# Hash attention and a gated feed-forward on one core: one token order for all batches, a longer hold on loads, and another end of the first and last block

## The chip, the cores and the metric

The kernel runs on one core of a Trainium2 chip. The metric is the device time of one execution in microseconds; before the change the median of five runs is 347.8 us (346.58 to 350.35). TensorE is called PE here, VectorE DVE, ScalarE ACT, GpSimd POOL and SyncE SP, as in the profile.

## The reference

```
B, H, S, D = 4, 8, 768, 64                       # q, k, v; proj is 64 x 6
q_bits = (einsum('bhsd,dk->bhsk', q, proj) > 0)  # the same for k
q_bucket = sum(q_bits * 2 ** arange(6), -1)
mask = q_bucket[:, :, :, None] == k_bucket[:, :, None, :]
scores = where(mask, matmul(q, k^T) / sqrt(D), -1e9)
attn = exp(scores - max); attn /= sum(attn) + 1e-9
x = (attn @ v).transpose(0, 2, 1, 3).reshape(3072, 512)
g = x @ w_gate                                   # 512 x 1536
ffn = (gelu(g) * (x @ w_val)) @ w_out
out = x + sigmoid(x @ w_res) * ffn
```

## The kernel before

**Tiles.** A batch has 768 tokens, six tiles of 128. Work goes by head pairs: 16 of them, n = 0 to 15, n = 4 b + j. For each pair, "aug" holds q and k transposed (64 rows) and under them seven rows made of the hash bits, so that one matmul over 71 rows gives score and mask together, and exp on ACT, with no maximum taken off, gives the weights. The matmul "attend" (L627) multiplies the weights with v, to which a column of ones is appended, so that the row sums come along; they collect in one PSUM tile "av" (a ring of one buffer) that has both heads of the pair side by side. DVE then takes the reciprocal of the sums (L640) and multiplies (L641) into "xtok", tokens by features.

**Blocks.** The queries are split in two halves, c = 0 and 1, of 384 tokens. A batch and a half make a block u = 2 b + c, eight in all. A block has 24 steps (`LB`): four head pairs, two heads, three pairs of key tiles (`steps`). Attention of block u runs woven with the feed-forward (`feed_forward`) of block u - 1: the value half (L697) with DVE's multiply (L700), then for each of three token tiles the residual gate (L709, tanh at L712) and the output (L721, then L730 and L733 on DVE and a store, L740). At the end of a block (`end_block`) the rest of that feed-forward is flushed, and then come twelve `gate` calls: four matmuls each (L681) and a gelu on ACT (L685), for which ACT loads another table.

**xT.** The feed-forward needs x transposed, "xT". In block 0 this is done by PE (L663, `transpose_x`) and a copy (L669), in the others by a DMA transpose of each head pair, issued on SP (L649) as soon as the pair's xtok is there. The gate takes its four contraction tiles, one for each head pair, in two parts, so that all but the last can begin before the last pair has arrived.

**Loads.** q, k, v of batch 0 come with tokens p*6+t (partition p, tile t), and its key tiles are taken in the order 0, 2, 4, 1, 3, 5 (`TS`). The pairs 4 to 15 are loaded by `load_blocks` on SP: four DMAs for q and four for k, each 32 columns of one head into 32 partitions (24 blocks of 32 tokens by 32 columns, 128 bytes a packet), and one for v. DVE turns each 32 by 32 block (L550), which makes the transpose. In these batches token t*128+p lies at partition p of tile t. POOL casts v (L403) and moves the hash bits by DMA (L568). Staging has three buffers each for q, k and v.

**Order.** Every operation is first listed by `op` with a cost, the keys that it reads and writes, and a place in the list. `arrange` then simulates the five engines and gives each the first listed operation that is ready. `urgent` moves an operation forward; `opens` and `closes` start and end a hold: while "xfer" is held, operations marked `held` on SP and POOL that are listed after the one that opened it aren't placed. It is opened by the exp of the seventh step from a block's end and closed by the block's last DMA transpose. For the loads the planner books 0.8 us of wire for a part of q or k and 1.8 for v. It also puts small matmuls into gaps of PE before 35 us (`keep_warm`, L850 and L853).

Of the kernel before, what the change touches and what calls it, by code (L numbers as in the profile page):

```python
# [11 lines left out]
FP32 = mybir.dt.float32  # L12
BF16 = mybir.dt.bfloat16
# [7 lines left out]
def kernel(  # L21
# [17 lines left out]
    P = 128  # L39
# [99 lines left out]
    def bank(dtype=FP32):  # L139
        return ring("mm", [P, 512 if dtype == FP32 else 1024], dtype, PSUM)  # L140
# [136 lines left out]
    def load(name, eng, queue, dst, cols, src, size, cost=0.5, held=False):  # L277
        queue_of = {"SP": nc.sync, "ACT": nc.scalar, "POOL": nc.gpsimd}
        op(eng, cost, lambda: queue_of[eng].dma_start(cols(dst()), src), r=[(name + "s", "gate")], w=[(dst, queue)],
           size=size, held=held)  # L280
# [18 lines left out]
    def load_blocks(n):  # L299

        b, j = pairs[n]
        for nm, src in (("q", q), ("k", k)):
            s = stage_of(nm, n, [P, S // Q, Q])
            for hh in range(2):
                for c in range(D // Q):
                    g = hh * D + c * Q
                    load(nm, "SP", g, s, lambda t, g=g: t[g:g + Q],
                         src[b, 2 * j + hh, :, c * Q:(c + 1) * Q].rearrange("(m p) d -> p m d", p=Q), 0.8, 0.85, True)
        s = stage_of("v", n, [P, 2, T, D])
        load("v", "SP", 0, s, lambda t: t, v[b, 2 * j:2 * j + 2].rearrange("h (t p) d -> p h t d", p=P), 1.8, held=True)  # L310


    for nm in "qk":
# [266 lines left out]
             for hh in range(2) for jp in range(T // 2)]  # L580
    LB = NPAIR * 2 * (T // 2)
    LEAD = 2
    URG, AVM = 200, 0.4
    PS = 2 * (T // 2)
    x_tok, xT, gh = {}, {}, {}
    e_tiles, av_tiles = {}, {}
# [2 lines left out]
    def scores(i):  # L589
        b, c, j, hh, jp = steps[i]  # L590
        n = b * NPAIR + j
        a = aug_of(n)[0:KAUG, hh, :]
        sp = ring("sc", [P, 2, 512], FP32, PSUM)
        e = e_tiles[i] = ring("e", [P, 2, CH], BF16)

        def emit():
            for x in range(2):
                jt = 2 * jp + x
                nc.tensor.matmul(sp()[:, x, 0:CH], a[:, S + jt * P:S + (jt + 1) * P],  # L599
                                 a[:, c * CH:(c + 1) * CH], start=True, stop=True)  # L600
        keys = [(0, c)] + sorted({(1, (2 * jp + x) // TC) for x in range(2)})
        op("PE", 0.325, emit, r=[("aug", n % NAUG, hh, side, p, kind) for side, p in keys for kind in "db"], w=[sp])
        op("ACT", 0.72, lambda: nc.scalar.activation(e(), sp()[:, :, 0:CH], AF.Exp, scale=EXPS),  # L603
           r=[sp], w=[e], table="exp", held=True, opens=("pair", i // PS) if i % PS == PS - 1 else None)
        if i % LB == LB - 1:
            ops[-1].opens = ("block", i // LB)
        if i % LB == LB - 7 and i // LB:
            ops[-1].opens = ("xfer", i // LB)

    def attend(i):  # L610
        b, c, j, hh, jp = steps[i]
        u = i // LB
        e = e_tiles.pop(i)
        first = hh == 0 and jp == 0
        last = hh == 1 and jp == T // 2 - 1
        if first:
            av_tiles[0] = ring("av", [P, 512], FP32, PSUM)
        av = av_tiles[0]
        va = vaugs[b % 2]

        def emit():
            live[:] = [] if last else [av]
            for x in range(2):
                jt = 2 * jp + x
                for t in range(TC):
                    o = (hh * TC + t) * DV
                    nc.tensor.matmul(av()[:, o:o + D + 1], e()[:, x, t * P:(t + 1) * P],  # L627
                                     va[:, 2 * j + hh, TS[b][jt], :],
                                     start=(first and x == 0 and t == 0), stop=(jt == T - 1),
                                     skip_group_check=True)  # L630
        op("PE", 0.18, emit, r=[e, ("vaug", b % 2, j)], w=[av], margin=AVM if first and u == 0 else 0.0)
        if last:
            if j == 0:
                x_tok[u] = ring("xtok", [P, NPAIR, TC, P], BF16)
            xt = x_tok[u]
            rec = ring("rec", [P, 2, TC, 1], FP32)

            def view():
                return av()[:, 0:2 * TC * DV].rearrange("p (h t d) -> p h t d", h=2, d=DV)
            op("DVE", 0.23, lambda: nc.vector.reciprocal(rec(), view()[:, :, :, D:D + 1]), r=[av], w=[rec], urgent=URG if u == 0 else 0)  # L640
            op("DVE", 0.56, lambda: nc.vector.tensor_mul(  # L641
                xt()[:, j].rearrange("p t (h d) -> p h t d", h=2),
                view()[:, :, :, 0:D], rec().to_broadcast([P, 2, TC, D])), r=[av, rec], w=[(xt, j)],
               closes=("pair", i // PS), urgent=URG if u == 0 else 0)
            if u:
                if j == 0:
                    xT[u] = ring("xT", [P, KM, CH], BF16)
                x = xT[u]
                op("SP", 1.25, lambda: nc.sync.dma_start_transpose(x()[:, j, :].rearrange("p (t n) -> p t n", n=P), xt()[:, j].rearrange("p t d -> p (t d)")),  # L649
                   r=[(xt, j)], w=[(x, j)], flight=2.0, closes=("xfer", u) if j == NPAIR - 1 else None)  # L650

# [21 lines left out]
    def gate(u, m):  # L673
        if m == 0:
            gh[u] = ring("gh", [P, KF, CH], BF16)
        g, x = gh[u], xT[u]
        ps = bank()
        for part in ((0, 1), (2, 3)) if u == 0 else ((0, 1, 2), (3,)):
            def emit(part=part):
                for kk in part:  # L680
                    nc.tensor.matmul(ps()[:, 0:CH], wg[:, kk, m * P:(m + 1) * P], x()[:, kk, :],  # L681
                                     start=(kk == 0), stop=(kk == KM - 1))
            op("PE", 0.163 * len(part), emit, r=[(key, kk) for kk in part for key in (x, "wg")], w=[ps],
               opens=("gelu", u) if m == 0 else None)
        op("ACT", 0.385, lambda: nc.scalar.activation(g()[:, m, :], ps()[:, 0:CH], AF.Gelu),  # L685
           r=[ps], w=[(g, m)], table="gelu", closes=("gelu", u) if m == 0 else None)

    def feed_forward(u):
# [14 lines left out]
        for t in range(TC):  # L703
# [11 lines left out]
            for h, W in enumerate(parts):  # L715
                cols = slice(sum(parts[:h]), sum(parts[:h]) + W)
                ps = bank()
                for k4 in range(KF // 4):
                    def emit(t=t, k4=k4, ps=ps, cols=cols, W=W):
                        for kk in range(4 * k4, 4 * k4 + 4):  # L720
                            nc.tensor.matmul(ps()[:, 0:W], g()[:, kk, t * P:(t + 1) * P], wo[:, kk, cols],  # L721
                                             start=(kk == 0), stop=(kk == KF - 1))
                    op("PE", 0.87 * W / DMODEL, emit, r=[(g, kk) for kk in range(4 * k4, 4 * k4 + 4)] + [("wo", gg) for gg in range(KF // 3)],
                       w=[ps], over=True)
                    if k4 < KF // 4 - 1:
                        yield 0.87
                z = "z" if len(parts) > 1 else ""
                y = ring("y" + z, [P, parts[0]], FP32)
                o = ring("o" + z, [P, parts[0]], FP32)
                op("DVE", 0.1 + 0.56 * W / DMODEL, lambda y=y, th=th, ps=ps, cols=cols, W=W: nc.vector.scalar_tensor_tensor(  # L730
                    y()[:, 0:W], th()[:, cols], 1.0, ps()[:, 0:W], op0=ALU.add, op1=ALU.mult), r=[th, ps], w=[y],
                   closes=("block", u + 1) if t == TC - 1 else None)
                op("DVE", 0.1 + 0.58 * W / DMODEL, lambda y=y, o=o, t=t, cols=cols, W=W: nc.vector.scalar_tensor_tensor(  # L733
                    o()[:, 0:W].rearrange("p (j d) -> p j d", d=P), y()[:, 0:W].rearrange("p (j d) -> p j d", d=P), 0.5,
                    xt()[:, cols.start // P:cols.stop // P, t, :], op0=ALU.mult, op1=ALU.add),
                   r=[y] + [(xt, j) for j in range(NPAIR)], w=[o])
                lay = "(p t) d -> p t d" if b == 0 else "(t p) d -> p t d"
                dst = out[b * S:(b + 1) * S, cols].rearrange(lay, t=T)[:, TS[b][c * TC + t], :]
                eng, queue = ("SP", nc.sync) if u == 2 * B - 1 else ("POOL", nc.gpsimd)
                op(eng, 0.6, lambda o=o, dst=dst, W=W, queue=queue: queue.dma_start(dst, o()[:, 0:W]), r=[o], size=0.8)  # L740
            yield 0.87
# [151 lines left out]
```

## Time and profile before

| | |
|---|---|
| five runs | 346.58, 346.87, 347.80, 349.71, 350.35 us |
| profiled execution | 346.87 us, span 345.1 us |
| PE clock | 1.00 throughout |
| PE, ACT, DVE, POOL busy | 98%, 68%, 56%, 18% of the span |
| DMA packets | 116357, of which 107802 under 512 bytes |
| DMA transposes | 28, 1.2 us each on SP when the queue is quiet |

The span runs from the first instruction to the last; the time of the execution holds 1.8 us more around it. Times in a timeline are microseconds from the start of the span. A line of a timeline has the start, the length (of all that is merged into it), engine, line, operation, tiles and count, and in brackets the idle time before it and what ended it.

### The profile page before, as it was taken

Reading aid. Unit: us, or ns where it says so; the run is one execution under the profiler, and the core shown is the slowest. Engines: PE = TensorE matmul, PEld = TensorE weight load, DVE = VectorE, ACT = ScalarE, POOL = GpSimd, SP = SyncE. Lnnn points to the kernel's source line nnn. Section 1 sums busy time; section 2 is a strip of 40 time slices with the busy share of each in tenths; the row PEclk is TensorE's granted clock in tenths of the full one; section 3 lists DMA queues with packets and bytes.
Section 4 is the critical chain, followed back from the end, with each engine's and each line's share of the span. In section 5 each row is a group of like instructions: output and inputs, shape, how many; then the busy total and the mean of one; then the engine's idle time right before and its main releaser. Section 6 shows DMA issues by size and latency. Waiting matters only on the chain.

```text
span 345.1 us, 7720 instructions
## 1 busy us (share of the span) xinstructions
PE 337.2 (98%) x3088; PEld 200.5 (58%) x3088; DVE 192.1 (56%) x344; ACT 234.2 (68%) x338; POOL 61.9 (18%) x107
## 2 busy tenths in 40 slices
PE   8999999989999999999999999999999999999996
PEld 3756666546555566555665556655666556655654
DVE  5997056977789738895453326725153314423353
ACT  4879887566766587666867758675877858775410
POOL 0444000540334310314011210203000100001000
PEclk9999999999999999999999999999999999999999
DMA  7999999999997399948200210111000120112002
GB/s 237 343 220 208 198 144 162 169 172 177 152 154 96 79 188 164 121 105 148 46 13 17 77 45 2 28 44 49 30 13 13 45 74 0 24 43 74 0 2 91
DMA packets 116357, 34.23 MB, mean 99 GB/s; under 512 B 107802, under 2 KB 113698, under 8 KB 116322
## 3 DMA queue, kind: packets, MB, share of 16 engines
q1 hardware_dynamic: 109522, 22.27, 42.3%
q0 software_dynamic: 6496, 11.27, 13.8%
q8 instruction: 24, 0.39, 0.5%
q10 hardware_dynamic: 304, 0.20, 0.2%
q14 instruction: 11, 0.09, 0.1%
HBM read 29.36 MB, written 6.29 MB: 103 GB/s over the span
## 4 chain that ended last, share of the span: by engine, by line
PE 87%; DVE 4%; DMA 4%; ACT 3%; issue 1%; DVEq 0%; ACTq 0%
PE mm L697 18%; PE mm L681 17%; PE sc L599 16%; PE mm L721 15%; PE av L627 9%; PE mm L709 5%; DMA xT<-xtok 4%; PE mm L558 3%; ACT e L603 2%; PE idle L850 1%; PE mm L481 1%; PE mm L518 1%; DVE bits L445 1%; PE mm L494 0%; DVE xtok L641 0%
## 5 line engine op out<-in xcount | busy, mean ns | idle before, releaser
L603 ACT ACTIVATE e<-sc 128x768 bf16<-128x768 f32 x192 | 149.9, 810 | 52.3 <-PE sc L599 51.9
L700 DVE TENSOR_TENSOR gh<-mm,gh 128x384 bf16<-128x384 f32 x96 | 53.4, 557 | 78.1 <-PE mm L697 62.8
L599 PE MATMUL sc<-aug 71*128 71x384 bf16 x384 | 92.3, 325 | 1.0 <-ACT e L603 0.9
L697 PE MATMUL mm<-xT,wv 128*128 128x384 bf16 x384 | 73.3, 326 | 0.0
L627 PEld LDWEIGHTS <-e 128*128 128x128 bf16 x1152 | 57.1, 97 | 24.3 <-issue 1.9
L721 PE MATMUL mm<-wo,gh 128*128 128x512 bf16 (+2 forms) x312 | 70.8, 363 | 0.0
L681 PE MATMUL mm<-xT,wg 128*128 128x384 bf16 x384 | 66.4, 326 | 1.8 <-DMA xT<-xtok 1.4
L685 ACT ACTIVATE gh<-mm 128x384 bf16<-128x384 f32 x96 | 45.5, 491 | 29.7 <-PE mm L681 29.5
L627 PE MATMUL av<-vaug,e 128*128 128x65 bf16 x1152 | 62.7, 193 | 0.6 <-DVE xtok L641 0.6
L681 PEld LDWEIGHTS <-wg 128*128 128x128 bf16 x384 | 36.9, 98 | 26.9 <-issue 2.7
L599 PEld LDWEIGHTS <-aug 71*128 71x128 bf16 x384 | 34.7, 98 | 28.7 <-issue 4.6
L697 PEld LDWEIGHTS <-wv 128*128 128x128 bf16 x384 | 34.0, 98 | 21.5 <-issue 3.1
L721 PEld LDWEIGHTS <-gh 128*128 128x128 bf16 x312 | 27.2, 98 | 24.6 <-issue 0.6
L730 DVE SCALAR_TENSOR_TENSOR y<-th,mm 128x512 f32<-128x512 bf16 x23 | 15.7, 684 | 43.6 <-PE mm L721 39.1
L568 POOL DMA_DIRECT2D aug<-bits x48 | 26.9, 564 | 67.5 <-DVE bits L565 66.8
L740 POOL DMA_DIRECT2D out_dram<-o x21 | 12.4, 592 | 133.3 <-DVE rec L640 112.6
L712 ACT ACTIVATE th<-mm 128x512 bf16<-128x512 f32 x24 | 14.3, 597 | 16.5 <-PE mm L709 16.5
L573 DVE TENSOR_SCALAR aug<-trT 64x1536 bf16<-64x1536 f32 x24 | 24.4, 1017 | 1.1 <-PE sc L599 0.4
L709 PE MATMUL mm<-wr,xT 128*128 128x512 bf16 x96 | 24.7, 379 | 0.0
L403 POOL CAST vaug<-vs 128x768 bf16<-128x768 f32 x16 | 13.3, 833 | 46.2 <-DMA vs<-in_v_dram 32.2
L565 DVE TENSOR_SCALAR bits<-mm,shift 128x384 bf16<-128x384 f32 x24 | 13.6, 609 | 9.7 <-PE mm L558 9.5
L641 DVE TENSOR_TENSOR xtok<-av,rec 128x384 bf16<-128x384 f32 x32 | 17.8, 557 | 1.1
(58 smaller groups left out, 166.6 us busy)
## 6 DMA issues: line engine op xcount, KB each, us to landing
vs<-in_v_dram SPq DMA_DIRECT2D x16, 384.0 KB
out_dram<-o POOLq DMA_DIRECT2D x21, 256.0 KB, 2.4
qs<-in_q_dram SPq DMA_DIRECT2D x48, 96.0 KB
ks<-in_k_dram SPq DMA_DIRECT2D x48, 96.0 KB
wg<-in_moe_w_gate_dram POOLq DMA_DIRECT2D x4, 384.0 KB, 7.4
wv<-in_moe_w_val_dram POOLq DMA_DIRECT2D x4, 384.0 KB, 8.1
wo<-in_moe_w_out_dram POOLq DMA_DIRECT2D x4, 384.0 KB, 12.5
qs<-in_q_dram SPq DMA_DIRECT2D x3, 384.0 KB
```

What stands on the lines that cost most here:

```text
L568: op("POOL", 0.6, lambda i=i: nc.gpsimd.dma_start(a[D:KAUG, :, i * CH:(i + 1) * CH], bits()[32 * i:32 * i + NR]), r=[(bits, 0), (bits, 1)] ...
L573: lambda hh=hh: nc.vector.tensor_scalar_mul(a[0:D, hh, :], trT()[hh * D:(hh + 1) * D].rearrange("d s n -> d (s n)"), QKS),
L599: nc.tensor.matmul(sp()[:, x, 0:CH], a[:, S + jt * P:S + (jt + 1) * P], a[:, c * CH:(c + 1) * CH], start=True, stop=True)
L603: op("ACT", 0.72, lambda: nc.scalar.activation(e(), sp()[:, :, 0:CH], AF.Exp, scale=EXPS), r=[sp], w=[e], table="exp", held=True, opens=(" ...
L627: nc.tensor.matmul(av()[:, o:o + D + 1], e()[:, x, t * P:(t + 1) * P], va[:, 2 * j + hh, TS[b][jt], :], start=(first and x == 0 and t == 0 ...
L641: op("DVE", 0.56, lambda: nc.vector.tensor_mul(xt()[:, j].rearrange("p t (h d) -> p h t d", h=2), view()[:, :, :, 0:D], rec().to_broadcast ...
L681: nc.tensor.matmul(ps()[:, 0:CH], wg[:, kk, m * P:(m + 1) * P], x()[:, kk, :], start=(kk == 0), stop=(kk == KM - 1))
L685: op("ACT", 0.385, lambda: nc.scalar.activation(g()[:, m, :], ps()[:, 0:CH], AF.Gelu), r=[ps], w=[(g, m)], table="gelu", closes=("gelu", u ...
L697: nc.tensor.matmul(ps()[:, 0:CH], wv[:, kk, m * P:(m + 1) * P], x()[:, kk, :], start=(kk == 0), stop=(kk == KM - 1))
L700: op("DVE", 0.46, lambda m=m, ps=ps: nc.vector.tensor_mul(g()[:, m, :], ps()[:, 0:CH], g()[:, m, :]), r=[ps], w=[(g, m)])
L709: nc.tensor.matmul(rps(), x()[:, kk, t * P:(t + 1) * P], wr[:, kk, :], start=(kk == 0), stop=(kk == KM - 1))
L721: nc.tensor.matmul(ps()[:, 0:W], g()[:, kk, t * P:(t + 1) * P], wo[:, kk, cols], start=(kk == 0), stop=(kk == KF - 1))
```

## The change

Loads of pairs 4 to 15 take tokens p*6+t, as batch 0 does; a part of q or k becomes a pattern of four indices, v one of longer rows, and the stores of all batches use the one pattern. The planner books 1.15 us of wire for v. In block 1 the hold "xfer" opens nine steps from the end in place of seven. In block 0, the last pair's reciprocal and multiply are done for each head as soon as it is there, and the planner tracks "av" by head. In the last block, the last pair is transposed on PE and copied by ACT or DVE, and the first two gates of that block take their PSUM from the ring of the scores. `SURG` is 0 and changes nothing.

```diff
-   load(nm, "SP", g, s, lambda t, g=g: t[g:g + Q],
-        src[b, 2 * j + hh, :, c * Q:(c + 1) * Q].rearrange("(m p) d -> p m d", p=Q), 0.8, 0.85, True)
+   load(nm, "SP", g, s, lambda t, g=g: t[g:g + Q].rearrange("p (t r) d -> p t r d", t=T),
+        src[b, 2 * j + hh, :, c * Q:(c + 1) * Q].rearrange("(r p t) d -> p t r d", p=Q, t=T), 0.8, 0.85, True)
-   load("v", "SP", 0, s, lambda t: t, v[b, 2 * j:2 * j + 2].rearrange("h (t p) d -> p h t d", p=P), 1.8, held=True)
+   load("v", "SP", 0, s, lambda t: t, v[b, 2 * j:2 * j + 2].rearrange("h (p t) d -> p h t d", t=T), 1.15, held=True)
...
+   XF = {1: 9}
-   if i % LB == LB - 7 and i // LB:
+   if i % LB == LB - XF.get(i // LB, 7) and i // LB:
        ops[-1].opens = ("xfer", i // LB)
...
-   op("PE", 0.18, emit, r=[e, ("vaug", b % 2, j)], w=[av], margin=AVM if first and u == 0 else 0.0)
-   if last:
+   op("PE", 0.18, emit, r=[e, ("vaug", b % 2, j)], w=[(av, hh)], margin=AVM if first and u == 0 else 0.0)
+   single = u == 0 and j == NPAIR - 1
+   if last or single and jp == T // 2 - 1:
...
+       heads = slice(hh, hh + 1) if single else slice(0, 2)
+       nh = heads.stop - heads.start
...
+       op("DVE", 0.18 + 0.025 * nh, lambda: nc.vector.reciprocal(rec()[:, 0:nh], view()[:, :, :, D:D + 1]),
+          r=[(av, h) for h in range(heads.start, heads.stop)], w=[rec], urgent=URG if u == 0 else 0)
+       op("DVE", 0.12 + 0.22 * nh, lambda: nc.vector.tensor_mul(
...
+   if u == 2 * B - 1 and j == NPAIR - 1:
+       ps = bank(BF16)
+       def emit():
+           for t in range(TC):
+               nc.tensor.transpose(ps()[:, t * P:(t + 1) * P], xt()[:, j, t, :], ident_bf)
+       op("PE", 0.2, emit, r=[(xt, j)], w=[ps])
...
+       op(None, {"DVE": 0.35, "ACT": 0.45}, evac, r=[ps], w=[(x, j)])
+       return
...
+   spare = u == 2 * B - 1 and m < 2
+   ps = ring("sc", [P, 2, 512], FP32, PSUM) if spare else bank()
...
-   lay = "(p t) d -> p t d" if b == 0 else "(t p) d -> p t d"
-   dst = out[b * S:(b + 1) * S, cols].rearrange(lay, t=T)[:, TS[b][c * TC + t], :]
+   dst = out[b * S:(b + 1) * S, cols].rearrange("(p t) d -> p t d", t=T)[:, TS[b][c * TC + t], :]
```

More of the change, by code (lines that the diff above doesn't have):

```diff
@@ L582 @@
     LEAD = 2
-    URG, AVM = 200, 0.4
+    XF = {1: 9}
+    URG, AVM, SURG = 200, 0.4, 0
     PS = 2 * (T // 2)
@@ L601, in scores @@
         keys = [(0, c)] + sorted({(1, (2 * jp + x) // TC) for x in range(2)})
-        op("PE", 0.325, emit, r=[("aug", n % NAUG, hh, side, p, kind) for side, p in keys for kind in "db"], w=[sp])
+        op("PE", 0.325, emit, r=[("aug", n % NAUG, hh, side, p, kind) for side, p in keys for kind in "db"], w=[sp],
+           urgent=SURG if i < LB else 0)
         op("ACT", 0.72, lambda: nc.scalar.activation(e(), sp()[:, :, 0:CH], AF.Exp, scale=EXPS),
@@ L635, in attend @@
             xt = x_tok[u]
+            heads = slice(hh, hh + 1) if single else slice(0, 2)
+            nh = heads.stop - heads.start
             rec = ring("rec", [P, 2, TC, 1], FP32)
             def view():
[L639 to L644, printed above, removed]
+                return av()[:, 0:2 * TC * DV].rearrange("p (h t d) -> p h t d", h=2, d=DV)[:, heads]
+            op("DVE", 0.18 + 0.025 * nh, lambda: nc.vector.reciprocal(rec()[:, 0:nh], view()[:, :, :, D:D + 1]),
+               r=[(av, h) for h in range(heads.start, heads.stop)], w=[rec], urgent=URG if u == 0 else 0)
+            op("DVE", 0.12 + 0.22 * nh, lambda: nc.vector.tensor_mul(
+                xt()[:, j].rearrange("p t (h d) -> p h t d", h=2)[:, heads],
+                view()[:, :, :, 0:D], rec()[:, 0:nh].to_broadcast([P, nh, TC, D])),
+               r=[(av, h) for h in range(heads.start, heads.stop)] + [rec], w=[(xt, j)] if last else [(xt, j, "half")],
+               closes=("pair", i // PS) if last else None, urgent=URG if u == 0 else 0)
+        if last:
+            xt = x_tok[u]
             if u:
@@ L648, in attend, with evac @@
                 x = xT[u]
+                if u == 2 * B - 1 and j == NPAIR - 1:
[4 more added lines that the diff above has]
+                    op("PE", 0.2, emit, r=[(xt, j)], w=[ps])
+                    def evac(e):
+                        copy = nc.scalar.copy if e == "ACT" else nc.vector.tensor_copy
+                        copy(x()[:, j, :], ps()[:, 0:CH])
+                    op(None, {"DVE": 0.35, "ACT": 0.45}, evac, r=[ps], w=[(x, j)])
+                    return
                 op("SP", 1.25, lambda: nc.sync.dma_start_transpose(x()[:, j, :].rearrange("p (t n) -> p t n", n=P), xt()[:, j].rearrange("p t d -> p (t d)")),
@@ L676, in gate, with acc @@
         g, x = gh[u], xT[u]
-        ps = bank()
+        spare = u == 2 * B - 1 and m < 2
+        ps = ring("sc", [P, 2, 512], FP32, PSUM) if spare else bank()
+        def acc():
+            return ps()[:, 0, 0:CH] if spare else ps()[:, 0:CH]
         for part in ((0, 1), (2, 3)) if u == 0 else ((0, 1, 2), (3,)):
@@ L680, in emit @@
                 for kk in part:
-                    nc.tensor.matmul(ps()[:, 0:CH], wg[:, kk, m * P:(m + 1) * P], x()[:, kk, :],
+                    nc.tensor.matmul(acc(), wg[:, kk, m * P:(m + 1) * P], x()[:, kk, :],
                                      start=(kk == 0), stop=(kk == KM - 1))
@@ L684, in gate @@
                opens=("gelu", u) if m == 0 else None)
-        op("ACT", 0.385, lambda: nc.scalar.activation(g()[:, m, :], ps()[:, 0:CH], AF.Gelu),
+        op("ACT", 0.385, lambda: nc.scalar.activation(g()[:, m, :], acc(), AF.Gelu),
            r=[ps], w=[(g, m)], table="gelu", closes=("gelu", u) if m == 0 else None)
```

## The prediction

> **What bounds the kernel now.** I read the page first. Its rows for one engine each, in tenths of 40 slices, say which engine is full where.
>
> ```profile
> span 345.1 us, 7720 instructions
> PE 337.2 (98%) x3088; PEld 200.5 (58%) x3088; DVE 192.1 (56%) x344; ACT 234.2 (68%) x338; POOL 61.9 (18%) x107
> PE   8999999989999999999999999999999999999996
> DVE  5997056977789738895453326725153314423353
> DMA  7999999999997399948200210111000120112002
> ```
>
> TensorE (PE) is busy everywhere; the DMA engines are full from the start to about 110 us and hardly used later. A full PE means that moving work on another engine is worth only the PE time that waits for it. So the second view is the waits of PE, all of them:
>
> ```profile
> PE mm L681 <- DMA xT<-xtok: 1.4, 1, 1.4
> PE idle L850 <- DVE proj_pair L332: 1.2, 1, 1.2
> PE sc L599 <- ACT e L603: 0.9, 3, 0.4
> PE av L627 <- DVE xtok L641: 0.6, 2, 0.3
> PE mm L681 <- ACT gh L685: 0.3, 1, 0.3
> ```
>
> These are gaps between records, and a record outlasts the issue of its matmul. One 384-column matmul is issued every 0.163 us (36 of L681 take 5.85 us in the chain of waits), though its record lasts 0.326. So I count lost issue time: start of the next matmul less start of the last, less 0.163. The timeline at the end of block 1 (the second boundary), PE and then the SP queue:
>
> ```profile
> 75.82 0.49 PE L681 MATMUL mm<-xT,wg 128*128 128x384 bf16 x2
> 77.73 1.79 PE L681 MATMUL mm<-xT,wg 128*128 128x384 bf16 x10 [1.42 <-DMA xT<-xtok]
> ...
> 64.42 2.32 SPq L279 DMA_DIRECT2D qs<-in_q_dram  x4
> 66.84 3.41 SPq L279 DMA_DIRECT2D ks<-in_k_dram  x4
> 70.37 0.46 SPq L279 DMA_DIRECT2D vs<-in_v_dram  x1
> 70.93 4.46 SPq L649 DMA_TRANSPOSE xT<-xtok  x2
> ```
>
> The second L681 starts at 75.99, the third was due at 76.15 and starts at 77.73: 1.58 us lost, to the DMA transpose of the last head pair. The same count at the other boundaries gives 0.23 at 160.2, 0.25 at 240.6, nothing at 118, 200 and 278, and 0.42 at the last one:
>
> ```profile
> 311.69 1.03 PE L709 MATMUL mm<-wr,xT 128*128 128x512 bf16 x4
> 312.55 2.75 PE L721 MATMUL mm<-wo,gh 128*128 128x512 bf16 x12
> 315.14 2.15 PE L681 MATMUL mm<-xT,wg 128*128 128x384 bf16 x12
> 317.54 0.65 PE L681 MATMUL mm<-xT,wg 128*128 128x384 bf16 x3 [0.25 <-ACT gh L685]
> ```
>
> There the last of twelve starts at 316.96, the next was due at 317.12 and starts at 317.54. From 36 us to the end this is all that PE loses to others, 2.5 us; whatever the change does there, it can't win more than 2.0 (both places it touches), 0.6%.
>
> **The load part.** A load of v goes from 1536 packets of 256 bytes to 256 of 1536. The trace has both: 256-byte packets on that queue took 23.9 ns in the mean, 1536-byte ones 71. On 16 engines that is 2.29 us against 1.14, 1.15 less for each of 12 loads. The loads of q and k keep their 6144 packets of 128 bytes a pair (18.2 ns, 7.0 us) in another order; their price in that order isn't in the trace. I take 18.2; the nearest rows bound it from 13.2 to 24.7, the lowest and highest means in 6-us stretches between 48 and 108 us, or 5.1 to 9.5 us a pair. A four-index source is what v has already, and its issue took 0.46 to 0.66 us, so issuing costs the same. None of this is on PE's path: the DMA engines run ahead, and the cover is the ring of three staging tiles. So 0, with v at 1.15 less a pair only thinning the traffic.
>
> By the Trainium skill ("DMA: Bandwidth & Descriptors", Why small descriptors are slow) a 256-byte descriptor costs 11 cycles, 3 of them overhead, so joining six would save under a quarter of v's wire time by an estimate from it, not half; the row decides, and the sum is 0 by either.
>
> The stores of batches 1 to 3 change from adjoining rows to every sixth, 2048 bytes each as before: 0.
>
> **The longer hold.** The exp that opens "xfer" in block 1 is now step 39, not 41, some 2.3 us earlier. Loads later in program order stay off SP until the block's last transpose is placed. The loads of pair 7 (listed at step 39, after its scores) are those at 64.42 to 70.83: nine DMAs, moved past the transposes of head pairs 2 and 3. Staging slots bound how many slip through: pair 7's q needs the slot of pair 4, transposed at 57.40 on DVE, and the hold opens near 60, so at most some three of nine go ahead.
>
> What that gives: pair 2's rows of xtok are done at 65.3 and needn't wait till 70.93; pair 3's are done at 72.97 and found SP in pair 2's transpose till 74.09, which took 3.15 us behind the loads instead of the 1.2 of a quiet queue. In the quiet boundary at 156 the chain shows 4.04 us from the end of DVE L641 to the landing. 72.97 + 4.05 = 77.02 instead of 77.69, so the third L681 starts 0.67 earlier: **-0.67**. Bounds: 0 if the landing stays where it is, -1.58 if DVE isn't held up by L733 ahead of L640 (it starts the reciprocal 0.7 late) and planned times fall well. What is late next: DVE, as 0.9 us of the wait stays.
>
> Where the moved loads go: they start at about 74.2, land by 74.2 + 8.1 + 3 = 85, then DVE 4, PE 0.8, POOL bits 2.3 and their landing 3.8 us: about 96, against the first use of pair 7 near 107 (step 66). Pairs 8 and later shift by some 8 us; pair 8 is first scored in block 4. So 0, covered by 11 us.
>
> **First block by head.** The last pair's reciprocal and multiply (0.20 + 0.56) become two of each. From L730's widths (512: 0.684, 256: 0.422, so 1.03 ns an element) a half multiply takes 0.36, so the tail is 0.20 shorter. But the tail isn't what PE waits for: the scores at 34.73 wait for ACT's exp that ends at 34.69, and the PE transposes follow them at 35.06, 0.2 after DVE ended. Gain 0 to 0.07. Against it stands a new wait. Both heads lie in one tile "av", and no row of before has DVE reading av while PE writes it; if DVE's read of head 0 orders the next av matmul behind it, PE waits. Head 0 ends at 31.70; DVE is then in a copy till 32.04, so its half ends at 32.3 or 32.65; the attend due at 32.17 comes at 32.45 or 32.8 (the hand-over of av took 0.14 at 30.52 to 30.66). Behind it stand fillers and the next scores, which then end at 33.24 to 33.57 for an exp due at 33.14: ACT, the bound there, loses 0.1 to 0.43. I take **+0.2**, bounds -0.1 and +0.45.
>
> The Trainium skill ("PSUM — Partial Sum Buffer", PSUM bank collisions) wants a bank guarded as a whole, not by address, which speaks for the wait; no overlap in this trace tests it. By it alone I would put +0.27, without it 0.
>
> **Last block on PE.** Three transposes at the 0.056 us of L663 (six in 0.34) add 0.17 on PE. They need xtok at 312.68 + 0.1; PE has L709 and four L721 till 313.41, so no wait. The copy out (0.35 to 0.55 as in L669, half as wide) hides behind the eight L721 that follow. The 0.42 goes, and m = 0, 1 take two score banks, idle by then. Removed from SP: one transpose with nothing behind it. **-0.42 + 0.17 = -0.25**; bounds +0.17 (the wait stays) and -0.25.
>
> **Sum.** -0.67 + 0.2 - 0.25 = -0.72. The profiled execution took 346.87 for its span of 345.1 (1.8 around it): 346.15. The median of the five runs lies 0.93 above it (346.58 to 350.35), and I can't see where the others lost that; if at the second boundary, it goes as well, if elsewhere, it stays (347.1). I say 346.5.
>
> **Rivals.**
> (1) The wait only changes hands: the landing is still late because DVE's L640 and L641 are, and the split costs its 0.4. Then -0.25 + 0.45 = +0.2: 347.1 to 347.5. For it: 0.9 of 1.58 is DVE's and the transpose's own time. Against: the SP rows show queueing of over 1 us.
> (2) Slower: DVE fills up in block 2. Pair 7's 3.85 us on DVE (two L550, two L573, at 80.02 to 83.83) leave the gate phase, where DVE is idle a third of the time, for the stretch 86 to 112, where it is busy 21.6 of 26: 25.4, 98%. The planner books 0.46 for L700, which takes 0.557: 12 x 0.097 = 1.2, and up to 0.7 for two L573. At full DVE this 1.9 falls on PE: 346.15 + 1.9 = 348.1; if all 3.85 do, 350.0. It decides once DVE passes about 98% in that stretch. Against it: pair 8's 3.9 us there aren't due until block 4 and can give way.
> (3) The hold does not bite, because the planner's queue runs ahead of the real one: 346.87 + 0.2 - 0.25 = 346.8. The slot of pair 4 speaks against it.
>
> **How the numbers follow.** Forecast 0.55, its own range 345.0 to 347.5; rival 1 0.17, rival 2 0.2, rival 3 0.08. The low end of the range is the floor, 346.87 - 1.58 - 0.25 - 0.1 = 344.9; the high end takes in half of rival 2, 348.9. A measurement of this kernel tells about 1% from no change; 1% faster (344.3) is under the floor and needs the spread of the runs to shrink too, 0.07; 1% slower (351.3) needs rival 2 in full and more, 0.08.
>
> **What would show it.** Right: SP has no q, k, v load between the transposes of head pairs 2 and 3 of block 1; the first of these is issued near 65 and lands before 70; PE's wait on xT falls from 1.4 to 0.3 to 0.9; the last boundary shows three transposes of L663's length and no wait on ACT. Wrong: a PE wait at L627 on DVE L641 or L640 over 0.5 near 32 us, PE waits on DVE between 86 and 112, or packets of 128 bytes well over 25 ns.

## The result and the profile after

The changed kernel takes 346.16 us (median of 43 executions, 345.44 to 347.32), the kernel before 347.17 (80 executions, 345.47 to 350.64); the ratio is 0.9962, 95% interval 0.995 to 0.9975. The ratios, here and below, are those on record over undisturbed executions, not quotients of the medians (here 0.9971), while medians and ranges are over all. The fastest executions of the two kernels are alike (345.44 and 345.47). What the change takes away most is the slow tail of before: 23 of 80 took more than 348 us, of the changed kernel none. The bulk moves less: the lower quartile is 346.63 before and 345.86 after.

The page of the changed kernel, as it was shown of before (a line of 40 digits has the tenths of 40 slices):

```profile
span 344.3 us, 7728 instructions
PE 337.6 (98%) x3091; PEld 200.8 (58%) x3091; DVE 191.1 (55%) x347; ACT 234.6 (68%) x338; POOL 62.4 (18%) x107
PE   8998999999999999999999999999999999999996
DVE  4998146864889638895464326725153414424353
DMA  7999998729995399826900210111000120111002
```

PE is as full as before, and the DMA engines show a hole in the ninth slice (69 to 77.5 us): the second boundary has lost its load traffic. All waits of PE:

```profile
PE idle L878 <- DVE proj_pair L332: 1.2, 1, 1.2
PE av L629 <- DVE xtok L648: 0.9, 3, 0.3
PE sc L600 <- ACT e L605: 0.9, 3, 0.4
PE mm L710 <- ACT gh L714: 0.2, 1, 0.2
```

The wait on xT, 1.4 us, is gone altogether; the attend (now L629) waits for DVE one time more. The second boundary, PE and then SP (L710 is the gate, L673 the DMA transpose):

```profile
75.99 1.14 PE L710 MATMUL mm<-xT,wg 128*128 128x384 bf16 x6
76.96 0.49 PE L600 MATMUL sc<-aug 71*128 71x384 bf16 x2
77.29 1.14 PE L710 MATMUL mm<-xT,wg 128*128 128x384 bf16 x6
...
66.49 1.21 SPq L673 DMA_TRANSPOSE xT<-xtok  x1
73.92 1.20 SPq L673 DMA_TRANSPOSE xT<-xtok  x1
75.17 1.31 SPq L279 DMA_DIRECT2D qs<-in_q_dram  x2
```

Head pair 2's transpose is issued at 66.49, 0.03 after its multiply ends and in 1.2 us, where it was issued at 70.93 and took 3.15; pair 3's at 73.92; pair 7's loads come after both. PE issues six gate matmuls, two scores and six gate matmuls without a gap.

The last boundary:

```profile
311.97 1.89 PE L750 MATMUL mm<-wo,gh 128*128 128x512 bf16 x8
313.70 0.33 PE L665 MATMUL mm<-ident_bf,xtok 128*128 128x128 bf16 x3
313.86 1.03 PE L750 MATMUL mm<-wo,gh 128*128 128x512 bf16 x4
314.73 1.46 PE L710 MATMUL sc<-xT,wg 128*128 128x384 bf16 x8
316.03 2.28 PE L710 MATMUL mm<-xT,wg 128*128 128x384 bf16 x13
```

The three transposes start 0.16 before the next group and the gates run through: the 0.42 before the thirteenth gate is gone.

### The profile page after: what moved, and what is told of

Its sections match the earlier page's. It is cut to its first block, busy times and chain, and to the rows that moved or that the text cites. A ratio compares the mean times of both kernels' runs of the same rounds, so it can differ in the third digit from the quotient of the medians.

```text
span 344.3 us, 7728 instructions
## 1 busy us (share of the span) xinstructions
PE 337.6 (98%) x3091; PEld 200.8 (58%) x3091; DVE 191.1 (55%) x347; ACT 234.6 (68%) x338; POOL 62.4 (18%) x107
## 4 chain that ended last, share of the span: by engine, by line
PE 93%; DVE 4%; ACT 1%; issue 0%; ACTq 0%; DVEq 0%
PE mm L726 18%; PE mm L750 18%; PE mm L710 17%; PE sc L600 17%; PE av L629 10%; PE mm L738 6%; PE mm L558 3%; PE idle L878 1%; PE mm L518 1%; PE mm L481 1%; ACT e L605 1%; DVE aug L455 1%; DVE aug L435 1%; PE mm L494 1%; DVE bits L445 1%; DVE xtok L648 1%
## 5 line engine op out<-in xcount | busy, mean ns | idle before, releaser
L629 PEld LDWEIGHTS <-e 128*128 128x128 bf16 x1152 | 57.2, 97 | 24.6 <-issue 2.2
L710 PE MATMUL mm<-xT,wg 128*128 128x384 bf16 x376 | 64.7, 326 | 0.2 <-ACT gh L714 0.2
L714 ACT ACTIVATE gh<-mm 128x384 bf16<-128x384 f32 x94 | 44.6, 491 | 27.9 <-PE mm L710 27.8
L629 PE MATMUL av<-vaug,e 128*128 128x65 bf16 x1152 | 62.7, 193 | 0.9 <-DVE xtok L648 0.9
L710 PEld LDWEIGHTS <-wg 128*128 128x128 bf16 x384 | 37.1, 98 | 25.1 <-issue 0.5
L741 ACT ACTIVATE th<-mm 128x512 bf16<-128x512 f32 x24 | 14.3, 597 | 16.6 <-PE mm L738 16.6
L403 POOL CAST vaug<-vs 128x768 bf16<-128x768 f32 x16 | 13.6, 850 | 65.1 <-DMA vs<-in_v_dram 59.6
L565 DVE TENSOR_SCALAR bits<-mm,shift 128x384 bf16<-128x384 f32 x24 | 13.6, 607 | 9.3 <-PE mm L558 9.2
L648 DVE TENSOR_TENSOR xtok<-av,rec 128x384 bf16<-128x384 f32 (+1 forms) x33 | 18.0, 545 | 1.1
```

Of the source, the lines that this page charges most:

```text
L648: op("DVE", 0.12 + 0.22 * nh, lambda: nc.vector.tensor_mul(xt()[:, j].rearrange("p t (h d) -> p h t d", h=2)[:, heads], view()[:, :, :, 0: ...
L710: nc.tensor.matmul(acc(), wg[:, kk, m * P:(m + 1) * P], x()[:, kk, :], start=(kk == 0), stop=(kk == KM - 1))
```

## The experiments

Lines in experiments made from the kernel before keep its numbers (L681 gate, L649 DMA transpose), those made from the changed kernel have the new ones. The experiments ran in three groups, in which the kernel before had a median of 346.91, 347.16 and 348.22 us; differences of some tenths of a microsecond between groups say little.

**One part at a time.** Theory A says that the hold does it all at the second boundary, theory B that the thinner traffic of the token order does.

hold_only, from the kernel before:

```diff
-        if i % LB == LB - 7 and i // LB:
+        if i % LB == LB - (9 if i // LB == 1 else 7) and i // LB:
```

> The kernel before with the hold of block 1 opened at step 39 and nothing else changed; in its program PE's order at the second boundary is the one of the changed kernel (six gate matmuls, two scores, six gate matmuls). Theory A (the hold alone takes away the wait of PE on xT at the second boundary, and that wait is also what spreads the runs of the kernel before from 345.5 to 350.6): median about 346.2 us, nothing above 348, no PE wait on xT near 76 us, 128-byte packets still near 18 ns. Theory B (the thinner load traffic of the new token order does it): 347.0 us, runs up to 350, a wait on xT of 1 us or more remains.

Measured: 346.20 us (345.30 to 346.71) beside 346.91 of the kernel before (345.94 to 350.44), ratio 0.996 (0.9933 to 0.9988). No wait near 76 us. 128-byte packets 17.0 ns.

layout_only, from the kernel before: the load, store and 1.15 lines of the diff alone.

> The kernel before with tokens p*6+t in all batches and 1.15 booked for v; hold as before, so PE's order at the second boundary is that of before (four scores, twelve attends, then twelve gate matmuls). Theory A: median about 347.0 us with runs up to 350, the wait of PE on xT near 76 us stays at 1 us or more. Theory B: 346.3 us and no runs above 348. Either way: v packets of 1536 bytes at 65 to 90 ns, 128-byte packets at 14 to 15 ns as in the changed kernel if their order makes them quicker, 18 if only the timing of the loads did.

Measured: 346.83 us (345.55 to 349.76), ratio 0.9968 (0.9934 to 1.0002). The wait stands:

```profile
76.06 0.49 PE L681 MATMUL mm<-xT,wg 128*128 128x384 bf16 x2
78.44 1.78 PE L681 MATMUL mm<-xT,wg 128*128 128x384 bf16 x10 [1.89 <-DMA xT<-xtok]
```

128-byte packets took 14.1 ns, v's 1536-byte ones 84.

no_hold, from the changed kernel:

```diff
-    XF = {1: 9}
+    XF = {}
```

> The changed kernel with the hold of block 1 back at seven steps. Theory A: the wait on xT near 76 us is back (1 to 1.6 us), median about 347.0 us and runs up to 350. Theory B: 346.2 us as the changed kernel, no spread.

Measured: 346.74 us (345.42 to 347.71), ratio to before 0.9965 (0.9938 to 0.9991). Theory A had 347.0, B 346.2; the median lies between and the spread comes back in part. Its profiled execution (345.81) shows a wait of 0.55 us at the second boundary. Together: the hold takes the wait away, as A says. It is worth 0.71 alone and 0.58 on top of the rest, between medians. The layout without the hold seems to thin the tail: 1 of 24 executions of layout_only and no_hold took over 348 us, against 23 of 80 before.

**What the wait is.** PE's order in the program of before at the second boundary, after four scores and twelve attends, is three gate matmuls for m = 0, three for m = 1, three for m = 2, and then the last ones. The wait stands before the third. That one needs head pair 2's transpose, not the last pair's. The chain of waits of the kernel before has it: its wait begins at 70.93, which is the issue of pair 2's transpose (pair 3's is issued at 74.19).

```profile
70.93 6.76 DMA xT<-xtok
77.73 1.79 PE mm L681 x10
```

But the hold also changes PE's order, because the planner sees pair 2 come sooner. Theory Q: the transpose stood in the queue; theory O: the other order is what helps.

hold_old_order, from hold_only:

```diff
             op("PE", 0.163 * len(part), emit, ...
+               margin=(0.5 if part == (3,) and m < 3 else 6.6 if m == 0 and part != (3,) else 0.0) if u == 1 else 0.0,
```

> hold_only with PE's order at the second boundary forced back to that of before (four scores, twelve attends, then gate matmuls 3, 3, 3, 1, 1): the planner is told that the first gate matmuls of block 1 become ready 6.6 us later and the last parts 0.5 us later. In the profiles so far the gate matmul that waits near 76 us is the third, which needs the transpose of head pair 2, not 3. Theory Q (pair 2's transpose stood in the queue behind pair 7's loads, and the hold takes it out from behind them): no wait at the third gate matmul; pair 3, landing near 78, may hold the tenth for up to 0.7 us; 346.2 to 346.9 us, nothing above 348. Theory O (the hold only helps because PE's order is another one): the third gate matmul waits 1.5 us or more again, 347.0 us, runs up to 350.

Measured: 346.49 us (345.52 to 346.97), ratio 0.9969 (0.9932 to 1.0005). The old order, no wait in it:

```profile
74.81 0.81 PE L599 MATMUL sc<-aug 71*128 71x384 bf16 x4
75.46 0.53 PE L627 MATMUL av<-vaug,e 128*128 128x65 bf16 x12
75.83 1.95 PE L681 MATMUL mm<-xT,wg 128*128 128x384 bf16 x11
```

early_old_queue, from the kernel before:

```diff
-                   r=[(xt, j)], w=[(x, j)], flight=2.0, ...
+                   r=[(xt, j)], w=[(x, j)], flight=-3.0 if u == 1 and j == 2 else 2.0, ...
```

> The kernel before, where the planner alone is told that pair 2's transpose of block 1 lands 5 us sooner: SP's order is as before (pair 7's loads ahead of the transpose), PE's order at the boundary is nearly that of the changed kernel (six gate matmuls right after the outputs). Theory Q: the third gate matmul is due about 1 us sooner and its data come no sooner: it waits 2.2 to 2.8 us; four scores less stand before it, so the time is as before or worse, 347.0 to 348.2 us, with runs up to 351. Theory O: no wait, 346.2 us.

Measured: median 348.83 us of ten executions, ratio 1.0012 (0.9968 to 1.0056). Nine took 345.31 to 350.60, one 1852.45, and why that one did is not known. The median is above what theory Q gave (347.0 to 348.2). PE, then SP:

```profile
75.29 0.49 PE L681 MATMUL mm<-xT,wg 128*128 128x384 bf16 x2
78.46 0.81 PE L681 MATMUL mm<-xT,wg 128*128 128x384 bf16 x4 [2.68 <-DMA xT<-xtok]
...
64.89 2.31 SPq L279 DMA_DIRECT2D qs<-in_q_dram  x4
67.31 3.49 SPq L279 DMA_DIRECT2D ks<-in_k_dram  x4
70.93 0.45 SPq L279 DMA_DIRECT2D vs<-in_v_dram  x1
71.48 4.23 SPq L649 DMA_TRANSPOSE xT<-xtok  x2
```

The new order with the old queue waits longer: the third gate is due at 75.62 and comes at 78.46, 2.84 us lost. The old order with the new queue doesn't wait, and none of its ten executions took over 347 us. Theory Q holds, O falls.

**Where the spread comes from.** Six profiled executions have pair 7's loads ahead of the transpose. The wait before the third gate, counted as issue time, against the time of the execution:

| kernel | wait, us | execution, us | difference |
|---|---|---|---|
| v_only | 0.00 | 345.28 | 345.28 |
| no_hold | 0.55 | 345.81 | 345.26 |
| before | 1.58 | 346.87 | 345.29 |
| layout_only | 2.05 | 347.08 | 345.03 |
| early_old_queue | 2.84 | 348.77 | 345.93 |
| qk_only | 3.34 | 349.19 | 345.85 |

In v_only 0.07 is lost at the tenth gate instead, which needs pair 3. The time moves by 3.9 us, the time less the wait by 0.9. So a wait of 0 to over 3 us, different in each execution, is most of what parts these six, and the executions of each version with the hold stay within 2 us of one another. That the slowest executions of the kernel before itself have this wait is inferred from the others: only one of its executions was profiled.

The wait is not the whole of the tail. Beside the experiments the kernel before ran 87 times. In 22 of these the granted clock was 0.989 to 0.995, and they took 348.56 to 351.24 us; in the other 65 it was 0.998 to 1.00, and they took 348.99 at most. Half a percent of 346 us is 1.7 us. No execution of a version with the hold has a clock under 0.998; of those without it, layout_only has one (349.76 us) and early_old_queue three (349.18 to 350.60). All six executions of the table had 1.00. So the longest times come with a lower clock, none of them was profiled, and whether a long wait of PE brings the lower clock is not shown.

**The split of the first block.** no_split, from the changed kernel, the planner's keys back to "av" as a whole:

```diff
-        single = u == 0 and j == NPAIR - 1
+        single = False
```

> The changed kernel with the last pair of the first block normalised in one piece, as before. If the split costs what the profile after shows (PE 0.50 us late at the attend near 32.6, no gain behind it): 0.2 to 0.4 us faster than the changed kernel, 345.8 to 346.0 us, and the first gate matmul 0.2 to 0.4 earlier after the first score than in the changed kernel. Rival (the shorter tail pays for the wait): same as the changed kernel, 346.1 to 346.3 us.

Measured: 345.59 us (344.76 to 345.90), ratio to before 0.9931 (0.9903 to 0.996): faster than the changed kernel. The two once more, on one chip:

> The version without the split once more, beside the changed kernel on the same chip. If the split costs what its wait and the rest of the first boundary show (0.4 to 0.8 us): 345.6 us, 0.4 to 0.8 below the changed kernel. Rival (the first comparison was the chip's): within 0.2 of it.

> The changed kernel itself, for that comparison: 346.2 us, nothing above 348.

Measured: 345.59 us (344.83 to 346.26) and 346.22 (345.33 to 347.00). The split costs 0.6 us. In the changed kernel, DVE and then PE:

```profile
32.07 0.55 DVE L693 COPY xT<-mm 128x768 bf16<-128x768 bf16 x1
32.62 0.18 DVE L646 RECIPROCAL rec<-av 128x3 f32<-128x3 f32 x1
32.84 0.36 DVE L648 TENSOR_TENSOR xtok<-av,rec 128x192 bf16<-128x192 f32 x1
...
33.25 0.34 PE L629 MATMUL av<-vaug,e 128*128 128x65 bf16 x6 [0.34 <-DVE xtok L648]
33.43 0.26 PE L881 MATMUL av<-aug 128*128 128x116 bf16 x2
...
35.30 0.73 PE L687 MATMUL mm<-ident_bf,xtok 128*128 128x128 bf16 x6
35.87 0.81 PE L710 MATMUL mm<-xT,wg 128*128 128x384 bf16 x4
```

Head 0's half ends at 33.20 and the attend of head 1 starts at 33.25, 0.50 later than PE's issue would have had it. The profile names DVE's multiply as what ended this wait, and it finds that by a semaphore: what is seen is an order that the program keeps, and what the memory would do without it is not shown. The second loss is in the transposes: 0.73 for six, where they take 0.50. They now stand straight behind the scores, and three of them wait 0.22 for DVE's second half (35.27 to 35.63). The third is at 38: PE loses 0.39 to a gelu, which stands behind ACT's table load at 36.69. Without the split the transposes have another score before them and run through:

```profile
34.66 0.48 PE L600 MATMUL sc<-aug 71*128 71x384 bf16 x2
35.40 0.48 PE L600 MATMUL sc<-aug 71*128 71x384 bf16 x2 [0.26 <-ACT e L605]
35.72 0.50 PE L687 MATMUL mm<-ident_bf,xtok 128*128 128x128 bf16 x6
```

PE loses 0.42 there, waiting for ACT, and nothing after. From the first score to the first gate of block 1 it is 65.63 and 65.61 us without the split (65.62 in hold_only), 66.44 and 66.78 with it (66.24 in dma_end).

split_three, from the changed kernel:

```diff
-        single = u == 0 and j == NPAIR - 1
+        single = u == 0 and j > 0
```

> The changed kernel with three pairs of the first block normalised by head in place of one (the last three). If each split makes PE's next attend wait for DVE's read of the other head's columns in the same tile: two more waits of 0.3 to 0.5 us at the fourth attend of a pair in the first block, and 0.3 to 0.8 us more to the first gate matmul, 346.6 to 347.6 us. Rival (the wait of 0.5 us at 32.6 was a chance of where DVE's copy stood): no such waits, 346.2 us.

Measured: 346.99 us (346.45 to 347.42), ratio to before 0.9985 (0.9951 to 1.0019). The attends that follow a split, and a change of pair between:

```profile
28.57 0.34 PE L629 MATMUL av<-vaug,e 128*128 128x65 bf16 x6 [0.34 <-DVE xtok L648]
31.88 0.52 PE L629 MATMUL av<-vaug,e 128*128 128x65 bf16 x12 [0.28 <-DVE xtok L648]
33.92 0.34 PE L629 MATMUL av<-vaug,e 128*128 128x65 bf16 x6 [0.37 <-DVE xtok L648]
```

28.57 and 33.92 are the attends of head 1 in the last two pairs, 0.50 and 0.53 of issue time late; 31.88 is the next pair's first, which waits for the single "av" as in the kernel before. In the first split pair head 1's attend starts at 22.80, 0.05 after the read ends, and no idle time is charged to it. Two more splits cost 0.8 us (346.99 against 346.16 to 346.22).

**The end.** dma_end, from the changed kernel: the transpose of the last pair back on SP, the first two gates back in the usual ring (both conditions replaced by False).

> The changed kernel with the last pair of the last block transposed by DMA as before, and its first two gates in the usual PSUM ring. Expected: the wait of 0.42 us on PE before the thirteenth gate matmul of the last block is back, three transposes (0.17) are gone, 0.25 us slower than the changed kernel, 346.4 us. Rival (the end was hidden anyway): 346.2 us.

Measured: 346.24 us (345.48 to 347.08), ratio to before 0.9958 (0.993 to 0.9987); beside 346.16 and 346.22 of the changed kernel the times can't tell. The profile can: the wait is back,

```profile
313.94 2.15 PE L710 MATMUL mm<-xT,wg 128*128 128x384 bf16 x12
316.34 0.97 PE L710 MATMUL mm<-xT,wg 128*128 128x384 bf16 x5 [0.25 <-ACT gh L714]
```

and from the first value matmul of the seventh block to the last matmul of PE it is 55.61 us, as in before, hold_only and hold_old_order, against 55.33 to 55.34 in the six profiles of kernels with the new end (after, after_again, no_split, no_split_again, no_hold, split_three): 0.28.

**Whose order makes the packets quicker.**

v_only and qk_only, from the kernel before: the one or the two load lines of the diff.

> The kernel before with the new token order in the loads of v alone, 1.8 still booked; v then meets keys of another order, so the attention of batches 1 to 3 is another computation; the instructions are the same. 128-byte packets of q and k took 18.2 ns in before and 14.1 with all of the layout. If v's 256-byte packets slowed them: 14 ns here. If their own order does it: 17 to 18.

> The kernel before with the new token order in the loads of q and k alone; v and the stores keep theirs, so the attention of batches 1 to 3 is another computation; the instructions are the same. If their own order makes the 128-byte packets quicker: 14 ns. If v's packets slowed them: 17 to 18.

Both read q and k in another token order than v, so they time the loads and leave the attention of the reference. Measured, one execution each: 16.6 ns with v's new order, 15.2 with that of q and k, against 18.2, 17.0, 16.8 and 17.7 in four profiles with neither and 13.6 to 15.1 in eight with both. Neither theory's number. The order of q and k takes off a part by itself; what v's order takes off is no more than the four profiles with neither differ among themselves.

## Why the prediction came out

**The total** was 346.15 by the sum and 346.5 as told, and 346.16 is measured. That is closer than its terms, and in part luck. The sum takes 0.72 off one execution, 346.87, that lies 0.30 under the median of 80 (347.17); the change took off 1.01 between the medians and 1.31 between the means (347.53 and 346.22). The split cost 0.4 more than booked, and the hold gave more.

**The hold** was booked at -0.67. Alone it gave 0.71 between the medians and 1.26 between the means (347.44 and 346.18), and from the first score to the start of PE's last matmul the profiles have 332.69 us in before and 331.27 in hold_only, 1.42 less. That the term is near the first of these is luck, for the step under it failed: the prediction put the wait on "the DMA transpose of the last head pair" and let 0.9 of 1.58 stay. The third gate waits for pair 2. Pair 3's transpose is issued at 73.92, hardly sooner than before (74.19), so by the prediction's path nearly all of the wait would have stayed. Pair 2's was what stood behind pair 7's loads, and with it 4.4 us sooner the whole 1.58 goes. The timeline had it: the first two gate matmuls had run, and their bank's third was late. Two things make the gain less than 1.58 in most executions: 0.42 comes back at 107 us, where a score of block 2 waits for ACT in the new order, and the profiled wait of 1.58 is one draw of a wait that varies. The bound of -1.58 was right as the floor of that one execution.

**The spread** was left open ("if at the second boundary, it goes as well"). It went with the hold, so the 0.35 added to the sum for it was not needed. The prediction had no word on the clock, which was lower in the slowest executions of before.

**The split** was booked at +0.2, with +0.45 as the end of its bounds, and costs 0.6. The wait at the attend was foreseen at 0.28 to 0.61 and is 0.50. The term that failed is what follows it: "PE transposes follow them at 35.06, 0.2 after DVE ended. Gain 0 to 0.07". In the new program the transposes stand before the second score, it seems because the planner counted on an earlier DVE; so they now wait for DVE, and the score, the exp and the gelu all come later. The rule of the Trainium skill ("PSUM — Partial Sum Buffer", PSUM bank collisions) that a bank be guarded as a whole, which by itself gave +0.27, agrees with the three head-1 attends that waited for the read of the other head's columns; it has no price for what the planner, which tracked the tile by head, made of the rest.

**The end** was booked at -0.25 and is 0.28 in the profile, step by step as told: transposes at 313.70 without a wait, the copy hidden.

**The loads.** At 0 they were within what layout_only can tell (0.9968, up to 1.0002). The packets were not as told: those of q and k got quicker, not the same, and v's long ones took 84 to 91 ns where 71 was booked, so that a load of v costs 256 x 89 / 16 = 1.42 us and saves 0.87 of 2.29, 38%. The row of 23.9 ns was itself a mixture: 10752 of its 29184 packets belong to the DMA transposes, whose 256-byte packets took 20.3 ns in the changed kernel, so v's own took about 26 by an estimate from these two, and the saving is 43%. The row had promised half. The estimate from the Trainium skill ("DMA: Bandwidth & Descriptors", Why small descriptors are slow) had given under a quarter, less than the 38% or 43% found.

**The rivals.** DVE (rival 2) was busy 23.0 of 26 us between 86 and 112, 88% and not 98%, because pair 8's transposes on DVE gave way, from 94.6 to 102.0, as the argument against it said; PE waited there for ACT alone. The hold did bite (rival 3): no load slipped between. Of rival 1 the second half came true, with the split at more than its 0.45.

## What to carry over

Before pricing a wait, follow the waiting instruction to its operand in program order: the wait was on the pair before the last, and by this trace a fix for the last one would have been worth little. A short transfer that PE needs soon must not be queued behind bulk loads that nobody needs for 30 us; its wait varies from run to run, so look at the spread of the times, and at the granted clock beside it, and not at one profile alone. And reading half of a PSUM tile early wasn't free here: the next write to the other half waited for it, so the version with the hold, the new token order and the PE transpose at the end, but without the split, is the best one here, 345.59 us.

## What the runs showed of the hardware that was not expected

The time of a 128-byte packet depends on the order of its addresses and on what else is in flight: 16.8 to 18.2 ns in the old order, 13.6 to 15.1 in the new, with the same count and size; the reason in the memory was not looked for. A long packet is slower in company: 1536 bytes took 71 ns where little but loads of the first batch ran, and 84 to 91 in the woven blocks. And a DMA transpose takes 1.2 us of SP's queue when the queue is quiet and 1.29 to 3.15 behind nine loads, in the five profiles where PE waited for it. In before it took 6.76 us from its issue to the landing (70.93 to 77.69) against 4.04 at a quiet boundary.
